# Masked attention with a rational feed-forward: scores as four 64-row products, the exponentials' sums in PSUM, fewer transfers, an order of its own

## The chip, the cores and the metric

The kernel runs on one core of a Trainium2 chip. The metric is device time in microseconds (us). The kernel before was timed three times: 1306.28 us in the median, 1305.25 to 1308.36. Engines are named as in the profile: PE is TensorE, DVE is VectorE, ACT is ScalarE, POOL is GpSimd, SP is SyncE, whose queue issues DMAs.

## The reference

Inputs are q, k and v of shape (8, 8, 576, 64): batch, heads, sequence, head size. All is float32.

```python
scores = scale * np.matmul(q, k.transpose(0, 1, 3, 2))
thresh = np.max(scores, axis=-1, keepdims=True) - tau
scores = np.where(scores >= thresh, scores, -1000000000.0)
scores = scores - np.max(scores, axis=-1, keepdims=True)
attn = np.exp(scores)
attn = attn / (np.sum(attn, axis=-1, keepdims=True) + 1e-09)
attn_out = np.matmul(attn, v)
...
x = np.ascontiguousarray(attn_out.transpose(0, 2, 1, 3)).reshape(B * S, H * D)
h = x @ w_in
P = a[0] + a[1] * h + a[2] * h * h + a[3] * h * h * h
Q = 1.0 + np.abs(b[0]) * np.abs(h) + np.abs(b[1]) * h * h
out = (P / (Q + 1e-06)) @ w_out
```

w_in is (512, 2048), w_out (2048, 512), and x has 4608 rows of 512. Only scores within tau of their row's maximum pass.

## The kernel before

**Units.** Two heads make a pair; there are 4 pairs in a batch and 32 in all. The 576 queries of a pair fall into four full tiles of 128 rows (t = 0 to 3) and a remainder of 64 (t = 4). A full unit is 128 queries of both heads against 576 keys; a remainder unit holds the 64 queries of both heads, one head in each half of the 128 rows. That makes 128 full units and 32 remainder units. A visit is a run of units of one pair: first tiles 0 and 1 of each pair of a batch, then tiles 2, 3 and the remainder on the way back. For each visit the transposed q and k of the pair are loaded into QQ and KK, two buffers of each (`load_ops`).

**A full unit's scores** (`f_qk`, L786 to L809). The first head's 64 channels lie on rows 0 to 63 of QQ and KK, the second head's on rows 64 to 127. Each head takes one product of 64 rows by 512 keys (L805). The last 64 keys of both heads are done in one product over all 128 rows (L809): KK holds two blocks of zeros, so that each head's queries meet only their own keys. The scores fill parts of three PSUM banks: bank 0 and the first 64 columns of bank 1 for the first head, the last 64 columns of bank 1 and bank 2 for the second. A PSUM bank has 512 float32 columns. In the trace a float32 product is two matmuls.

**Behind the scores.** DVE takes the two row maxima (L815). L822 or L824 makes the threshold. ACT reads the scores out of PSUM, head by head, with a function that throws the scores below the threshold far down (L830), and then gives the three banks back: the operation is planned at L956 with the hold on the banks to drop. ACT takes the exponential in SBUF, and the sum of each row with it (L834); the profile shows the reading of that sum as an instruction of its own, ACTIVATION_READ_ACCUMULATOR. The sum goes to a small SBUF tile, st. L839 (on ACT) or L841 (on DVE) scales it, and L845 inverts it. Then the weights are split into a high and a low float16 part (L339/L341 and L856), transposed by a DMA of SP's queue (L866) and multiplied by v (L925). In the first batch the transposes run on TensorE instead (L879, L884, L909).

**Banks.** The first 21 units choose between two sets of banks, (0, 1, 2) and (3, 4, 5); from the 22nd on all have the one set (0, 1, 2). Banks 3 to 5 are then the accumulators and work banks of the feed-forward, 5 to 7 its other work banks.

**Feed-forward.** Steps of 256 rows of x by 512 of the 2048 middle columns (`moe_ops`): L1042 multiplies by w_in, L1051 takes the result out of PSUM, the rational function runs on DVE (L1062 to L1084) and ACT (L1056, L1069, L1072), and L1101 multiplies by w_out. They run beside the score units of later batches, and the last ones by themselves.

**The order** is written out by the program. Each operation is given to a planner (`Plan`) with an engine, or two to choose from, a duration, a key, what it comes after, and what buffers or banks it takes and drops. The planner goes through a model of time, at each step starts the operation that can start soonest, and among those that are level, the one with the smallest key. The keys come from the unit's position, and from two lists of numbers, TURN (one per unit or step) and KIND (one per sort of operation). PRICE and EARLY weigh ACT against DVE where both could do the work. Every engine then does its instructions in the order in which the plan has put them; semaphore waits between engines follow from the tiles that instructions share.

**Loads.** The q and k of the first two batches are issued from SP's queue (k of the first two pairs from ACT's), those from the third batch on from POOL's queue. A q load is three transfers (L650 to L652), a k load is three (L657 to L659), and two more in a visit with a remainder (L662).

Of the kernel before, what the change touches and what calls it, by code (L numbers as in the profile page):

```python
# [16 lines left out]
AX = mybir.AxisListType  # L17

# [27 lines left out]
NQ = 2  # L46
# [4 lines left out]

FROM_ACT = 2
# [25 lines left out]
EARLY = {"ACT": 1.2900, "DVE": 3.3863}  # L78
EARLY_END = 714.5248
PRICE = {"ACT": 1.0645, "DVE": 2.1978}  # L80

TURN = [
# [21 lines left out]
KIND = [  # L104
# [8 lines left out]
LOADS_END = 120.0  # L113
# [22 lines left out]
class Plan:  # L136
# [20 lines left out]
    def op(self, eng, dur, key, fn, after=(), take=(), drop=()):  # L157
        engs = {eng: dur} if isinstance(eng, str) else eng
        o = Op(engs, key, fn, [x for x in after if x is not None], list(take), list(drop))
        o.turn, o.kind = self.turn, self.kinds.setdefault(fn.__code__, len(self.kinds))  # L160
# [26 lines left out]
    def order(self):  # L187
# [19 lines left out]
        left = len(self.ops)  # L207
        while left:
# [38 lines left out]
            if e == "DMA" and o.drop and t < LOADS_END:  # L247

                o.dur = 2.0 * o.dur + 1.0
            free[e] = end = t + o.dur  # L250
            busy[e] += o.dur
            seen = end + self.LAT[e]
            for h in o.take:
# [18 lines left out]
            for d in o.then:  # L272
                d.wait -= 1
                for x in d.engs:
                    d.ready[x] = max(d.ready[x], end + (self.OWN[e] if x == e else self.TO.get((e, x), self.LAT[e])))
                    if not d.wait:
                        can[x].append(d)
# [12 lines left out]
def masked_attention_rational_ffn(  # L290
# [86 lines left out]
    QW = S + REM  # L377
    QQs = [const.tile([P, QW], F32, name=f"QQ{i}") for i in range(NQ)]
    KKs = [const.tile([P, QW + REM], F32, name=f"KK{i}") for i in range(NQ)]
    for t in QQs:  # L380
        nc.gpsimd.memset(t[:, NT * P:], 0.0)
    for t in KKs:
        nc.gpsimd.memset(t[0:D, S:QW], 0.0)
        nc.gpsimd.memset(t[D:P, 0:REM], 0.0)
# [96 lines left out]
    def decode_ops(i, key, load, hold, dst=None):  # L481
# [6 lines left out]
        def ld():  # L488
            if not loaded:

                for x in KKs[0][:, REM:REM + 1], QQs[0][:, 0:1]:
                    nc.gpsimd.tensor_scalar(cf[:, 15:16], x, 1.0, 1.0, ALU.mult, ALU.mult)
# [32 lines left out]
        l = op("GD", 2.5, key - 2.0, ld, (), [hold])  # L525
# [112 lines left out]
    def load_ops(bp, ts):  # L638
# [7 lines left out]
        queue, eng = (nc.sync, "DMA") if bp < EARLY_BP else (nc.gpsimd, "GD")  # L646

        def ldq():
# [3 lines left out]
            queue.dma_start(QQ[D:P, S:], qT[bb, pr, :, S:S + REM])  # L652

        def ldk():
            KK = KKs[kh.slot]
            kq_ = nc.scalar if bp < FROM_ACT else queue
            kq_.dma_start(KK[0:D, REM:S], kT[bb, pr, :, 0:NT * P])  # L657
            kq_.dma_start(KK[D:P, REM:QW], kT[bb, pr, :, S + REM:])
            kq_.dma_start(KK[0:D, 0:REM], kT[bb, pr, :, NT * P:S])  # L659
            if NT in ts:  # L660
                for i in range(2):
                    kq_.dma_start(KK[i * D:(i + 1) * D, QW:], kT[bb, pr, :, NT * P + i * REM:S + i * REM])  # L662

        q_done[bp] = [op(eng, 4.3 if first else 1.6, p0, ldq, (), [qh])]
        k_done[bp] = [op(eng, 0.1 if bp < FROM_ACT else 1.6, p0 + 0.1, ldk, (), [kh])]

# [13 lines left out]
    def load_v_ops(bp):  # L680
# [25 lines left out]
        l = v_loaded[bp] = op(eng, 1.6, max(q, V0 + V1 * pr), ld, (), [vhold])  # L706
# [56 lines left out]
    def unit_ops(bp, t):  # L763
# [3 lines left out]
        single = units.index((bp, t)) < SINGLE  # L767
# [18 lines left out]
        def f_qk():  # L786
# [5 lines left out]
            if not full:  # L792

                s = box["s"][0] = s[:, 0:S]
                for k0, c0, n in (REM, 0, NT * P), (QW, NT * P, REM):
                    nc.tensor.matmul(s[:, c0:c0 + n], QQ[:, NT * P:QW], KK[:, k0:k0 + n], **one)
# [4 lines left out]
            for hh in range(2):  # L801

                r = slice(hh * D, (hh + 1) * D)
# [480 lines left out]
```

## Time and profile before

| | |
|---|---|
| median of three runs | 1306.28 us |
| the profiled execution | 1312.41 us |
| its span, first to last instruction | 1310.6 us |
| mean granted TensorE clock | 0.986 |
| PE busy | 1253.8 us (96%) |
| DVE busy | 1217.9 us (93%) |
| ACT busy | 1114.4 us (85%) |
| POOL busy | 243.4 us (19%) |
| full units' 512-wide products, L805 | 154.0 us, 512 matmuls |
| full units' shared product, L809 | 63.3 us, 256 matmuls |
| exponentials, L834 | 222.1 us, 288; reading their sums 58.1 us, 288 |

Busy time is the union of an engine's instructions. Those of TensorE overlap, and their ends are modelled, so starts tell more than lengths there. In a row of the timeline stand the start, the length, the engine, the line, the operation, what it writes and reads, the shape and the count; in a row of groups the count is followed by busy time, mean ns of one, and the idle time of the engine ahead of them with what ended it.

### The profile page before, as it was taken

To read this page: it belongs to the slowest core of one execution; us is meant where nothing else is said; L and a number is where in the kernel's file an instruction comes from. 1 tells how busy PE (TensorE), PEld (TensorE's weight loads), DVE (VectorE), ACT (ScalarE), POOL (GpSimd) and SP (SyncE) were. 2 spreads that over 40 slices of the span, in tenths; PEclk is the share of its full clock that TensorE was granted. 3 is DMA by queue.
4 is the path that set the end of the run, shared out by engine and by line. 5 is a ranking of instruction groups with operands and counts; after the bars stand their busy time and mean duration, and the time that the engine had idled before them with its cause. 6 is when DMAs were issued, how large, how long until landed. Compare 5 with 4: busy or idle time off the path is not lost. (4 is left out here: it accounts for less than half of the span.)

```text
span 1310.6 us, 25351 instructions
## 1 busy us (share of the span) xinstructions
PE 1253.8 (96%) x9430; PEld 931.8 (71%) x9430; DVE 1217.9 (93%) x1913; ACT 1114.4 (85%) x2182; POOL 243.4 (19%) x462
## 2 busy tenths in 40 slices
PE   8898989999999999998999979999999999999998
PEld 6576677777677777776777657766677777778886
DVE  5899999999999999988999979999999999999777
ACT  5898998999999999997999878978998798885564
POOL 1101100023213220323112231223213221110000
PEclk8998999999999999999999989999999999999999
DMA  7433454476656565677554875676756654563000
GB/s 206 132 116 125 142 128 87 105 160 119 124 116 134 124 131 107 117 143 129 95 103 96 115 132 100 122 126 119 137 106 115 132 131 75 109 111 55 17 17 17
DMA packets 340587, 146.66 MB, mean 112 GB/s; under 512 B 316208, under 2 KB 323184, under 8 KB 340464
## 3 DMA queue, kind: packets, MB, share of 16 engines
q1 hardware_dynamic: 316400, 86.49, 37.4%
q0 software_dynamic: 22784, 57.31, 16.4%
q8 instruction: 74, 1.21, 0.4%
q10 hardware_dynamic: 1280, 1.25, 0.4%
q14 instruction: 49, 0.40, 0.1%
HBM read 60.30 MB, written 9.44 MB: 53 GB/s over the span
## 5 line engine op out<-in xcount | busy, mean ns | idle before, releaser
L1101 PE MATMUL banks<-wp,g 128*128 128x512 f32 x1728 | 442.1, 404 | 1.6 <-DVE g L1092 1.2
L1042 PEld LDWEIGHTS <-wi 128*128 128x128 f16 x3456 | 333.6, 98 | 67.1 <-issue 29.0
L1042 PE MATMUL banks<-x,wi 128*128 128x256 f16 x3072 | 360.8, 274 | 10.0 <-ACT t L1051 9.3
L1101 PEld LDWEIGHTS banks<-wp,g 128*128 128x128 f32 x1728 | 315.9, 189 | 75.3 <-DVE g L1092 4.0
L834 ACT ACTIVATE e<-e,cf 128x576 f32<-128x576 f32 x288 | 222.1, 778 | 0.2
L856 DVE SCALAR_TENSOR_TENSOR e<-e,st,hi 128x576 f16<-128x576 f32 x252 | 204.6, 812 | 7.5 <-ACT hi L339 6.4
L339 ACT ACTIVATE hi<-e,st 128x576 f16<-128x576 f32 x223 | 169.6, 769 | 46.8 <-DVE st L845 30.8
L830 ACT ACTIVATE e<-banks,st 128x576 f32<-128x576 f32 x288 | 206.3, 737 | 3.0 <-DMA pT<-e 0.8
L815 DVE TENSOR_REDUCE st<-banks 128x2 f32<-128x1152 f32 x128 | 172.4, 1347 | 16.2 <-PE banks L809 15.8
L805 PE MATMUL banks<-KK,QQ 64*128 64x512 f32 x512 | 154.0, 650 | 7.2 <-DVE t L346 3.9
L925 PE MATMUL banks<-pT,V 128*64 128x256 f16 (+1 forms) x2520 | 122.8, 250 | 12.8 <-DMA pT<-e 10.2
L1051 ACT ACTIVATE t<-banks,hsc 128x512 f32<-128x512 f32 (+1 forms) x192 | 106.1, 574 | 30.3 <-PE banks L1042 24.5
L925 PEld LDWEIGHTS <-V 128*64 128x64 f16 x2520 | 105.0, 111 | 34.0 <-issue 22.7
L809 PEld LDWEIGHTS banks<-KK,QQ 128*128 128x128 f32 x256 | 38.6, 190 | 99.1 <-issue 94.6
L1078 DVE SCALAR_TENSOR_TENSOR t<-t,co,t 128x1024 f32<-128x1024 f32 (+1 forms) x73 | 92.3, 1265 | 17.4 <-ACT t L1072 17.1
L1069 ACT ACTIVATE t<-t,co 128x1024 f32<-128x1024 f32 (+1 forms) x73 | 82.8, 1134 | 29.6 <-DVE t L1065 24.1
L1092 DVE TENSOR_TENSOR g<-t,g 128x512 fp32r<-128x512 f32 x144 | 95.0, 684 | 3.1 <-ACT g L331 2.9
L650 POOL DMA_DIRECT2D QQ<-in_qT_dram x42 | 22.2, 529 | 381.0 <-PE banks L809 194.8
L1084 DVE SCALAR_TENSOR_TENSOR t<-t,co,t 128x1024 f32<-128x1024 f32 (+1 forms) x73 | 92.3, 1265 | 0.6
L1075 DVE SCALAR_TENSOR_TENSOR t<-t,co,t 128x1024 f32<-128x1024 f32 (+1 forms) x73 | 92.2, 1264 | 0.1
L1065 DVE SCALAR_TENSOR_TENSOR t<-t,co 128x1024 f32<-128x1024 f32 (+1 forms) x73 | 92.3, 1264 | 0.0
L1062 DVE SCALAR_TENSOR_TENSOR t<-t,co 128x1024 f32<-128x1024 f32 (+1 forms) x73 | 92.2, 1263 | 0.0
(128 smaller groups left out, 1545.3 us busy)
## 6 DMA issues: line engine op xcount, KB each, us to landing
t<-in_w_in_dram POOLq DMA_DIRECT2D x16, 512.0 KB, 5.3
t<-in_w_out_dram POOLq DMA_DIRECT2D x16, 512.0 KB, 4.1
out_dram<-u POOLq DMA_DIRECT2D x26, 256.0 KB, 2.9
V<-in_v_dram POOLq DMA_DIRECT2D x24, 256.0 KB, 4.5
QQ<-in_qT_dram POOLq DMA_DIRECT2D x42, 144.0 KB, 2.8
KK<-in_kT_dram POOLq DMA_DIRECT2D x42, 144.0 KB, 3.2
QQ<-in_qT_dram POOLq DMA_DIRECT2D x42, 128.0 KB, 2.9
KK<-in_kT_dram POOLq DMA_DIRECT2D x42, 128.0 KB, 2.8
```

Source lines behind the costliest of these rows:

```text
L339: nc.scalar.activation(dst, src, AF.Identity, scale=factor)
L805: nc.tensor.matmul(d, QQ[r, t * P:(t + 1) * P], KK[r, REM:S], **one)
L815: nc.vector.tensor_reduce(box["st"][:, 0:2], box["both"], AX.X, ALU.max, negate=True)
L830: nc.scalar.activation(ev(hh), box["s"][hh], AF.Prelu, scale=SCALE, bias=box["st"][:, 2 + hh:3 + hh], alpha=STEEP)
L834: nc.scalar.activation(e, e, AF.Exp, scale=passes, accum_out=box["st"][:, 4 + hh:5 + hh])
L856: nc.vector.scalar_tensor_tensor(box["lo"][:, c], ev(hh), box["st"][:, 6 + hh:7 + hh], box["hi"][:, c], ALU.mult, ALU.subtract)
L925: nc.tensor.matmul(dst, V[:, c * P + hh * D:c * P + (hh + 1) * D], rhs, start=c == 0 and n == 0, stop=c == NT and n == 2)
L1042: nc.tensor.matmul(d, wi_tile(c, f0 + j, hl), x[:, c, :], start=c == 0 and n == 0, stop=c == NC - 1 and n == 2)
L1051: nc.scalar.activation(box["h3"][:, 2 * k:2 * k + 2, sl], psv[:, :, sl], AF.Identity, scale=hsc[:, b2, g:g + 1])
L1065: nc.vector.scalar_tensor_tensor(box["q"], box["q"], bc, box["q"], ALU.add, ALU.mult)
L1092: nc.vector.tensor_tensor(fr(g[:, 1]), box["r"][:, k * GW:(k + 1) * GW], g[:, 0], ALU.subtract)
L1101: nc.tensor.matmul(acc[tt], fr(g[:, x]), fr(wo[f][y]), start=begins and j == n == 0, stop=ends and j == nb - 1 and n == 2)
```

## The change

A full unit's scores are made by four products of 64 rows: the first head's last 64 keys (bank 1), the second head's first 512 (bank 2), the first head's first 512 (bank 0), the second head's last 64 (bank 1). Ahead of the last stands an empty instruction on TensorE that waits for the first. KK no longer has blocks of zeros, and its four memsets go. The remainder unit keeps its two products over all rows.

From the 22nd unit on the sum of the exponentials goes to bank 1, in columns 64 to 79, two for each of eight units in turn, and L839/L841 read it from there.

K is loaded by two transfers, one for each head, whole. Q is loaded by two, and a third in visits with a remainder. ACT's queue issues only the first visit's k of the first two pairs. The queues of q and k are as before otherwise: SP for the first two batches, POOL from the third on.

TURN, KIND, EARLY and PRICE have other values. The planner counts a transfer's landing in another way (`wire`), and two durations are other numbers: a full unit's products 1.36 for 1.47, an exponential 0.735 for 0.76.

```diff
-EARLY = {"ACT": 1.2900, "DVE": 3.3863}
+EARLY = {"ACT": 1.2754, "DVE": 3.5364}
-PRICE = {"ACT": 1.0645, "DVE": 2.1978}
+PRICE = {"ACT": 1.0661, "DVE": 2.2744}
...
-    QW = S + REM
-    KKs = [const.tile([P, QW + REM], F32, name=f"KK{i}") for i in range(NQ)]
-    for t in KKs:
-        nc.gpsimd.memset(t[0:D, S:QW], 0.0)
-        nc.gpsimd.memset(t[D:P, 0:REM], 0.0)
+    KKs = [const.tile([P, S], F32, name=f"KK{i}") for i in range(NQ)]
...
+        act = bp < FROM_ACT and ts[0] == 0
-            queue.dma_start(QQ[D:P, S:], qT[bb, pr, :, S:S + REM])
+            if NT in ts:
+                queue.dma_start(QQ[D:P, S:], qT[bb, pr, :, S:S + REM])
...
-            kq_ = nc.scalar if bp < FROM_ACT else queue
-            kq_.dma_start(KK[0:D, REM:S], kT[bb, pr, :, 0:NT * P])
-            kq_.dma_start(KK[D:P, REM:QW], kT[bb, pr, :, S + REM:])
-            kq_.dma_start(KK[0:D, 0:REM], kT[bb, pr, :, NT * P:S])
-            if NT in ts:
-                for i in range(2):
-                    kq_.dma_start(KK[i * D:(i + 1) * D, QW:], kT[bb, pr, :, NT * P + i * REM:S + i * REM])
+            kq_ = nc.scalar if act else queue
+            for hh, c in (0, 0), (1, S + REM):
+                kq_.dma_start(KKs[kh.slot][hh * D:(hh + 1) * D, :], kT[bb, pr, :, c:c + S])
...
-            for hh in range(2):
+            for hh, k0, n, d0 in (0, NT * P, REM, NT * P), (1, 0, NT * P, w - NT * P), (0, 0, NT * P, 0), (1, NT * P, REM, w - S):
                 r = slice(hh * D, (hh + 1) * D)
-                d = s[:, 0:NT * P] if hh == 0 else s[:, w - NT * P:]
-                nc.tensor.matmul(d, QQ[r, t * P:(t + 1) * P], KK[r, REM:S], **one)
-
-            dst, src = (bass.AP(x.tensor, x.offset, [list(x.ap[0]), [n, 2], [1, REM]])
-                        for x, n in ((s[:, NT * P:S], w - 2 * NT * P - REM), (KK[:, 0:REM], S)))
-            nc.tensor.matmul(dst, QQ[:, t * P:(t + 1) * P], src, **one)
+                if d0 == w - S:
+                    tc.add_manual_dep(nc.tensor.nop().ins, shared.ins.name, ORDERED, reason="one bank")
+                mm = nc.tensor.matmul(s[:, d0:d0 + n], QQ[r, t * P:(t + 1) * P], KK[r, k0:k0 + n], **one)
+                if d0 == NT * P:
+                    shared = mm
...
+        def total(h0, h1):
+            if single:
+                return box["st"][:, 4 + h0:4 + h1]
+            o = S - 512 + 2 * (place_of[bp, t] % 8)
+            return ps[:, 1, o + h0:o + h1]
...
-            nc.scalar.activation(e, e, AF.Exp, scale=passes, accum_out=box["st"][:, 4 + hh:5 + hh])
+            nc.scalar.activation(e, e, AF.Exp, scale=passes, accum_out=total(hh, hh + 1))
...
-                nc.scalar.activation(r, box["st"][:, 4:4 + nh], AF.Copy, scale=UP, bias=1e-9 * UP)
+                nc.scalar.activation(r, total(0, nh), AF.Copy, scale=UP, bias=1e-9 * UP)
-                nc.vector.tensor_scalar(r, box["st"][:, 4:4 + nh], 1e-9, UP, ALU.add, ALU.mult)
+                nc.vector.tensor_scalar(r, total(0, nh), 1e-9, UP, ALU.add, ALU.mult)
...
-        qk = op("PE", 1.47 if full else 1.12, p, f_qk, need, [sh[0]], [kh, qh] * nh)
+        qk = op("PE", 1.36 if full else 1.12, p, f_qk, need, [sh[0]], [kh, qh] * nh)
...
-            mk[hh] = op("ACT", 0.76, p + 0.3 + 0.02 * hh, lambda hh=hh: f_sum(hh), [ex[hh]])
+            mk[hh] = op("ACT", 0.735, p + 0.3 + 0.02 * hh, lambda hh=hh: f_sum(hh), [ex[hh]])
```

More of the change, by code (lines that the diff above doesn't have):

```diff
@@ L50 @@
 EARLY_BP = 8
+EARLY_QK = 8
 FROM_ACT = 2
@@ L206, in order @@
         done, busy = [], dict.fromkeys(engines, 0.0)
-        left = len(self.ops)
+        left, wire = len(self.ops), 0.0
         while left:
@@ L252, in order @@
             seen = end + self.LAT[e]
+            if o.wire is not None:
+                wire = max(wire, t + BEGIN) + o.wire[0]
+                seen = max(wire, end + 1.0) + o.wire[1]
             for h in o.take:
@@ L274, in order @@
                 for x in d.engs:
-                    d.ready[x] = max(d.ready[x], end + (self.OWN[e] if x == e else self.TO.get((e, x), self.LAT[e])))
+                    d.ready[x] = max(d.ready[x], seen if o.wire is not None else
+                                     end + (self.OWN[e] if x == e else self.TO.get((e, x), self.LAT[e])))
                     if not d.wait:
@@ L374, in masked_attention_rational_ffn @@
     ones = bass.AP(one.tensor, one.offset, [list(one.ap[0]), [0, P]])
-    QW = S + REM
-    QQs = [const.tile([P, QW], F32, name=f"QQ{i}") for i in range(NQ)]
-    KKs = [const.tile([P, QW + REM], F32, name=f"KK{i}") for i in range(NQ)]
+    QQs = [const.tile([P, S + REM], F32, name=f"QQ{i}") for i in range(NQ)]
     for t in QQs:
         nc.gpsimd.memset(t[:, NT * P:], 0.0)
-    for t in KKs:
-        nc.gpsimd.memset(t[0:D, S:QW], 0.0)
-        nc.gpsimd.memset(t[D:P, 0:REM], 0.0)
+    KKs = [const.tile([P, S], F32, name=f"KK{i}") for i in range(NQ)]
     nc.vector.tensor_scalar(passes, cf[:, 6:7], 0.0, None, ALU.is_ge)
@@ L489, in ld @@
             if not loaded:
-                for x in KKs[0][:, REM:REM + 1], QQs[0][:, 0:1]:
+                for x in KKs[0][:, 0:1], QQs[0][:, 0:1]:
                     nc.gpsimd.tensor_scalar(cf[:, 15:16], x, 1.0, 1.0, ALU.mult, ALU.mult)
@@ L523, in f6 @@
                 tensor_tensor(dst.bitcast(I32), t, box["rw"][:, :, 0], ALU.add)
-        l = op("GD", 2.5, key - 2.0, ld, (), [hold])
+        l = op("GD", 2.5, key - 2.0, ld, (), [hold], wire=(1.75, 2.0))
         if i < NC:
@@ L645, in load_ops @@
         p0 = p - (4.6 if first else 4.0)
-        queue, eng = (nc.sync, "DMA") if bp < EARLY_BP else (nc.gpsimd, "GD")
+        act = bp < FROM_ACT and ts[0] == 0
+        queue, eng = (nc.sync, "DMA") if bp < EARLY_QK else (nc.gpsimd, "GD")
         def ldq():
@@ L651, in ldq @@
             queue.dma_start(QQ[D:P, 0:NT * P], qT[bb, pr, :, S + REM:])
-            queue.dma_start(QQ[D:P, S:], qT[bb, pr, :, S:S + REM])
+            if NT in ts:
+                queue.dma_start(QQ[D:P, S:], qT[bb, pr, :, S:S + REM])
         def ldk():
-            KK = KKs[kh.slot]
-            kq_ = nc.scalar if bp < FROM_ACT else queue
-            kq_.dma_start(KK[0:D, REM:S], kT[bb, pr, :, 0:NT * P])
-            kq_.dma_start(KK[D:P, REM:QW], kT[bb, pr, :, S + REM:])
-            kq_.dma_start(KK[0:D, 0:REM], kT[bb, pr, :, NT * P:S])
-            if NT in ts:
-                for i in range(2):
-                    kq_.dma_start(KK[i * D:(i + 1) * D, QW:], kT[bb, pr, :, NT * P + i * REM:S + i * REM])
-        q_done[bp] = [op(eng, 4.3 if first else 1.6, p0, ldq, (), [qh])]
-        k_done[bp] = [op(eng, 0.1 if bp < FROM_ACT else 1.6, p0 + 0.1, ldk, (), [kh])]
+            kq_ = nc.scalar if act else queue
+            for hh, c in (0, 0), (1, S + REM):
+                kq_.dma_start(KKs[kh.slot][hh * D:(hh + 1) * D, :], kT[bb, pr, :, c:c + S])
+        issue = {"DMA": 1.25, "GD": 1.1}[eng]
+        q_done[bp] = [op(eng, 3.1 if first else issue + (0.6 if NT in ts else 0.0), p0, ldq, (), [qh], wire=(0.75, 1.0))]
+        k_done[bp] = [op(eng, 0.1 if act else issue, p0 + 0.1, ldk, (), [kh], wire=(0.75, 1.0))]
+    place_of = {u: i for i, u in enumerate(units)}
     def is_plain(bp, t):
@@ L705, in load_v_ops @@
         q = bp * (NT + 0.5) - 17.0
-        l = v_loaded[bp] = op(eng, 1.6, max(q, V0 + V1 * pr), ld, (), [vhold])
+        l = v_loaded[bp] = op(eng, 1.7, max(q, V0 + V1 * pr), ld, (), [vhold], wire=(0.95, 1.5 if eng == "DMA" else 2.5))
         hv = [Hold("u", 1)]
@@ L766, in unit_ops @@
         full = t < NT
-        single = units.index((bp, t)) < SINGLE
+        single = place_of[bp, t] < SINGLE
         heads = (0, 1) if full else (0,)
@@ L794, in f_qk @@
                 s = box["s"][0] = s[:, 0:S]
-                for k0, c0, n in (REM, 0, NT * P), (QW, NT * P, REM):
-                    nc.tensor.matmul(s[:, c0:c0 + n], QQ[:, NT * P:QW], KK[:, k0:k0 + n], **one)
+                for c0, n in (0, NT * P), (NT * P, REM):
+                    nc.tensor.matmul(s[:, c0:c0 + n], QQ[:, NT * P:], KK[:, c0:c0 + n], **one)
                 return
@@ L982, in unit_ops @@
             tp = op("DMA", TPD if full else 0.6 * TPD, p + 0.6, lambda: f_tp("hi"), his + two["tp"], [two["pT"]] if t % 2 == 0 else (),
-                    [hi_hold])
-            tp = op("DMA", TPD if full else 0.6 * TPD, p + 0.65, lambda: f_tp("lo"), los + [tp], (), [e_hold])
+                    [hi_hold], wire=(1.2 if full else 0.65, 0.8))
+            tp = op("DMA", TPD if full else 0.6 * TPD, p + 0.65, lambda: f_tp("lo"), los + [tp], (), [e_hold], wire=(1.2 if full else 0.65, 0.8))
             two["tp"].append(tp)
```

10 lines of the change are left out of this document (5 added, 5 removed), and 50 rows, old and new, of tables (KIND, TURN).

## The prediction

> **What bounds the kernel now.** First the page, for the balance of the engines:
>
> ```profile
> span 1310.6 us, 25351 instructions
> ...
> PE 1253.8 (96%) x9430; PEld 931.8 (71%) x9430; DVE 1217.9 (93%) x1913; ACT 1114.4 (85%) x2182; POOL 243.4 (19%) x462
> ...
> DVE 19%; ACT 4%; issue 4%; PE 2%; DMA 1%; ACTq 0%; DVEq 0%
> ```
>
> The chain of waits reaches back only over 30% of the span, and VectorE holds 19 of those 30 parts; but TensorE is as full. So I cut the span into start, middle and tail with the view of busy time by stretch (columns: PE, its weight loads, DVE, ACT, POOL):
>
> ```profile
> 0.00:200.00 200.00, 177.57 (x1232) 130.31 (x1233) 174.38 (x391) 172.37 (x374) 22.52 (x58) 0.96 0.49 139
> 200.00:1200.00 1000.00, 970.75 (x7542) 715.27 (x7542) 959.26 (x1438) 881.63 (x1712) 220.90 (x404) 0.99 0.61 117
> 1200.00:1311.00 111.00, 105.49 (x659) 86.23 (x657) 84.25 (x86) 60.44 (x97) 0.00 (x0) 1.00 0.05 15
> ```
>
> In the 1000 us in which score units and feed-forward steps run side by side, TensorE is idle for 29 us, VectorE for 41, ScalarE for 118. Two engines have next to no slack, all work in the order that the program wrote, and a new wait of a microsecond per unit finds no room. What one unit does there, by the timeline of each engine (start, length):
>
> ```profile
> 600.34 0.30 ACT L822 ACTIVATE st<-st,cf 128x2 f32<-128x2 f32 x1
> 600.67 1.37 ACT L830 ACTIVATE e<-banks,st 128x576 f32<-128x576 f32 x2
> 601.93 0.77 ACT L834 ACTIVATE e<-e,cf 128x576 f32<-128x576 f32 x1
> 602.60 0.20 ACT L834 ACTIVATION_READ_ACCUMULATOR e<-e,cf 128x1 f32 x1
> 602.69 0.77 ACT L834 ACTIVATE e<-e,cf 128x576 f32<-128x576 f32 x1
> 603.36 0.19 ACT L834 ACTIVATION_READ_ACCUMULATOR e<-e,cf 128x1 f32 x1
> 603.45 1.14 ACT L1069 ACTIVATE t<-t,co 128x1024 f32<-128x1024 f32 x1
> ```
>
> ```profile
> 602.84 1.13 PE L805 MATMUL banks<-KK,QQ 64*128 64x512 f32 x4
> 603.90 0.49 PE L809 MATMUL banks<-KK,QQ 128*128 128x128 f32 x2
> 604.14 2.34 PE L1101 MATMUL banks<-wp,g 128*128 128x512 f32 x9
> ```
>
> ```profile
> 604.49 0.16 DVE L841 TENSOR_SCALAR st<-st 128x2 f32<-128x2 f32 x1
> 604.69 0.17 DVE L845 RECIPROCAL st<-st 128x2 f32<-128x2 f32 x1
> 604.77 1.34 DVE L815 TENSOR_REDUCE st<-banks 128x2 f32<-128x1152 f32 x1
> ```
>
> From the 22nd unit on there is one set of score banks (0, 1, 2). ScalarE empties it with L830 (ends 602.04); the next unit's products enter it at 602.84, while the exponentials of the unit before still run (the second ends at 603.55) and before its sums are read (L841, 604.49). Today that is free, since the sums lie in an SBUF tile.
>
> **The change, part by part.**
>
> *Sums in bank 1.* The exponential of unit n (L834) now writes its sum into bank 1, into which unit n+1's two 64-wide products write and from which its maximum reads; L839/L841 read the sum from there. The diff itself makes one of the 64-wide products wait for the other, with the reason "one bank"; I take it that sums and products, which share that bank on two engines, are kept in program order as well. Then a product that stands behind the sums in the program waits for them, and a sum that stands behind the product waits for the product. How often would they meet? Over 138 successions of units on the single set, I compared the start of a unit's first product with the end of the sums before it: in 121 the product is the earlier, by 0.83 us in the median and 127 us in all. The first and the last:
>
> ```profile
> 171.34 1.35 PE L805 MATMUL banks<-KK,QQ 64*128 64x512 f32 x4
> ```
>
> ```profile
> 174.40 0.83 ACT L834 ACTIVATE e<-e,cf 128x576 f32<-128x576 f32 x1
> 175.06 0.25 ACT L834 ACTIVATION_READ_ACCUMULATOR e<-e,cf 128x1 f32 x1
> ```
>
> ```profile
> 1179.35 1.19 PE L796 MATMUL banks<-KK,QQ 128*128 128x512 f32 x4
> ```
>
> ```profile
> 1179.37 0.76 ACT L834 ACTIVATE e<-e,cf 128x576 f32<-128x576 f32 x1
> 1180.04 0.19 ACT L834 ACTIVATION_READ_ACCUMULATOR e<-e,cf 128x1 f32 x1
> ```
>
> Bounds of the wait on TensorE: none, where the new order keeps them apart; 127 us, where every product stands behind both sums. In between: if a product that now starts before the second sum stands ahead of that sum in the program, it waits for the first alone. By the same comparison that makes 75 us on TensorE, and 64 us on ScalarE for the second sums that then wait for the product. I take 75, because the planner's list knows nothing of this wait: the score banks are still given back by L830 (the hold that L956 drops), and the exponential takes no hold on them. Queued behind the waiting product on TensorE are the feed-forward matmuls (L1101 from 604.14 above), and VectorE's L1062 to L1092 wait for those. TensorE's own 29 us of idle time take some of it; ScalarE's 64 us fit into its 118. On the path: 75 - 29 = +46 us (bounds 0 and 127).
> The Trainium skill, page "PSUM — Partial Sum Buffer", section "PSUM bank collisions raise a hardware error", says that accesses by two engines have to be guarded by bank and quarter of the partitions, and not by address, reads included. By that rule the different columns of the sums are no protection, and the wait is certain; by addresses alone it would be nothing. No row here shows two engines on different columns of one bank.
>
> *Four products.* Today a full unit takes TensorE from 602.84 to 604.14, 1.30 us; before a feed-forward step of the other layer it is 1.39:
>
> ```profile
> 194.33 1.13 PE L805 MATMUL banks<-KK,QQ 64*128 64x512 f32 x4
> 195.39 0.49 PE L809 MATMUL banks<-KK,QQ 128*128 128x128 f32 x2
> 195.72 0.38 PE L1042 MATMUL banks<-x,wi 128*128 128x256 f16 x2
> ```
>
> A float32 product is two passes; the 64-row pairs run side by side, four records in 1.06 us, 0.53 a pass. The new unit has on each half of the rows two 512-wide passes and two 64-wide ones. No row shows a 64-row, 64-wide pass. The nearest is the remainder unit on all rows:
>
> ```profile
> 244.40 0.65 PE L796 MATMUL banks<-KK,QQ 128*128 128x512 f32 x2
> ```
>
> ```profile
> 243.97 1.19 PE L796 MATMUL banks<-KK,QQ 128*128 128x512 f32 x4
> 245.00 0.38 PE L1042 MATMUL banks<-x,wi 128*128 128x256 f16 x2
> ```
>
> There a 512-wide pass takes 0.43, and the two 64-wide ones what is left of 1.03: 0.17, or 0.085 each. If the 64-row form adds the 0.10 that it adds to a 512-wide pass, 0.185. So the new unit takes 1.06 + 0.17 to 1.06 + 0.37, 1.23 to 1.43, against 1.30 to 1.39: from -0.11 to +0.08 a unit, times 128 units -14 to +10 us. I take the middle, -2. The wait for the first 64-wide product is over long before the other half has done its 1.06 us.
> The Trainium skill, page "TensorE: Matmul & The Clock Gate", part "Packing small matmuls — row/col tiling", says that a weight load overlaps running matmuls only on other rows. The 0.53 against 0.43 agrees, and by that rule the part would gain nothing.
>
> *The sum's own price.* A pass with a sum takes 0.76 (601.93 to 602.69), one without 0.69 (half of 1.37): at most 0.07 times 288 = 20 us of ScalarE's time, at least nothing. I take 8, and on the path -1, since ScalarE has 118 us to spare. The 45 sums read on VectorE may cost as much more as the nearest small bank read does:
>
> ```profile
> 608.80 0.23 DVE L941 SCALAR_TENSOR_TENSOR xr<-banks,xr 128x64 f16<-128x64 f32 x1
> ```
>
> 0.23 against 0.16, 45 times: +3 us of VectorE, +1 on the path.
>
> *Fewer transfers.* K goes from three or five issues a visit to two, Q from three to two, three in a visit with a remainder; on GpSimd:
>
> ```profile
> L662 POOL DMA_DIRECT2D KK<-in_kT_dram x48 | 26.0, 552 | 0.2 <-issue 0.2
> L652 POOL DMA_DIRECT2D QQ<-in_qT_dram x42 | 22.7, 540 | 0.0
> L659 POOL DMA_DIRECT2D KK<-in_kT_dram x42 | 22.5, 535 | 1.8 <-DMA V<-in_v_dram 1.7
> ...
> L650 POOL DMA_DIRECT2D QQ<-in_qT_dram x42 | 22.2, 529 | 381.0 <-PE banks L809 194.8 <-PE banks L796 181.8 <-PE banks L1101 4.4
> ```
>
> Of these the 48, the 42 of L659 and 18 of L652 go, some 58 us of issuing, but the queue stood idle for 381 us ahead of L650 until TensorE gave a buffer back: hidden by the visit in work, two buffers deep. Without that cover it would be about two issues, 1.1 us, for each of 42 visits. In the first batch the second visits of two head pairs move from ScalarE's queue to SP's, and on GpSimd four memsets of K go:
>
> ```profile
> 1.34 0.61 ACTq L658 DMA_DIRECT2D KK<-in_kT_dram  x1
> 1.48 0.59 SPq L650 DMA_DIRECT2D QQ<-in_qT_dram  x1
> 1.54 0.14 POOL L383 MEMSET KK<- 64x64 f32 x1
> ...
> 8.41 1.13 PE L805 MATMUL banks<-KK,QQ 64*128 64x512 f32 x4
> ```
>
> Ten issues of 0.61 leave ScalarE in the first 200 us (28 us idle there), four of 0.59 join SP, where transposes queue behind them; the memsets lie seven microseconds ahead of the first product. All of it together I count as -1 us (bounds -6, all ten issues on the path, and +2, the four on SP's).
>
> *Own order.* Bounds from the idle time: it can win back at most TensorE's 29 us and lose any amount; I take -2.
>
> **Sum.** 46 - 2 - 1 + 1 - 1 - 2 = +41 on the span of 1310.6, 1351.6. The profiled execution took 1312.4, 1.8 more than its span, and the median of the runs is 1306.3, 0.5% below it: (1351.6 + 1.8) x 0.9953 = 1347; I say 1345.
>
> **The rivals.**
> *Kept apart (faster).* Place: the bank between L830 and the next product. The new order puts other matmuls ahead of each product and the sums straight behind L830, so no wait is seen, and the products and the sums' price give what they can: -14 and half of the 8, 1288; two thirds of it, 1294. For it: in 17 of 138 successions the sums are over in time already. Against: the list does not know that they must be. It decides once the waits for sums stay under the 29 us that TensorE has to spare.
> *Full chain (far slower).* Every product stands behind both sums, and bank 1 goes from product to maximum to L830 to sums and back, one owner at a time: 127 - 29 - 5 = +93, 1399. For it: L834 starts straight behind L830 in the rows above, and so stands early in the program. It decides where the product is planned later than the second sum in most units; today that is 74 of 138.
> *Products in file.* If the passes start only in program order, the second head's last wide pass starts at 0.53, the first head's two wide passes behind it at 0.53 and 1.06, and the unit ends near 1.6 instead of 1.30 to 1.39: +0.21 to 0.3, times 128 at least +27 us: 1333, with no wait for sums. The four records in 1.06 speak against it, since two pairs ran side by side, with the first head's second pass behind the second head's first. The Trainium skill's page on TensorE, in the part named above, says that matmuls start and end in program order, which would be this case if it held for each pass.
> *Nothing.* The change is off the path at both ends: 1306.
>
> **How the numbers follow.** Forecast (waits for the sums, 1310 to 1375 by itself) 0.38; full chain 0.11; in file 0.06: slower 0.55. Kept apart 0.38: faster. Nothing 0.07: same. A change under 0.2% can't be told from none. The range 1291 to 1390 leaves out the best of "kept apart" and the worst of "full chain".
>
> **What would show it.** Right: L805's first product preceded by idle time on TensorE that ends with ScalarE's L834, some 0.5 us each, tens of us in all; or L834 preceded by idle time that ends with TensorE's products. Wrong: neither row, with L830 still followed by L834 within 0.1 us and TensorE's idle time between 200 and 1200 us still near 29. The four products: 1.23 to 1.43 us to the next matmul, 1.6 if in file. A sum's pass below 0.76 shows its price. POOL's idle time ahead of its Q transfers stays in the hundreds.

## The result, and the profile after

The changed kernel takes 1432.32 us (median of four runs, 1428.70 to 1436.69) beside 1305.76 for the kernel before: a ratio of 1.0967 with a 95% interval of 1.0932 to 1.1002, or 127 us more. The forecast was 1345, with a range that ended at 1390. It had the sign, and the size was missed threefold. The changed file has other line numbers: the four products are L807, the remainder's L797, the exponential L840, the sums' scaling L845 (ACT) and L847 (DVE), the reciprocal L851, the feed-forward's products L1048 and L1107.

The page of the changed kernel first, its span, engines and chain of waits:

```profile
span 1430.2 us, 25976 instructions
...
PE 1266.7 (89%) x9716; PEld 977.4 (68%) x9716; DVE 1223.8 (86%) x1918; ACT 1129.6 (79%) x2178; POOL 185.6 (13%) x349
...
PE 14%; ACT 9%; DVE 6%; issue 4%; DMA 1%; POOL 1%; ACTq 0%; DVEq 0%; POOLq 0%
```

The work hardly grew: TensorE 13 us more than before, VectorE 6, ScalarE 15. The span grew by 120. So it is idle time, and the view of busy time by stretch (columns as in the prediction) shows that all engines have it:

```profile
200.00:1200.00 1000.00, 878.41 (x6845) 667.85 (x6843) 857.95 (x1283) 803.87 (x1536) 155.42 (x282) 0.97 0.54 105
```

In the same 1000 us, into which less of the work now fits, TensorE idles for 122 us (29 before), VectorE for 142 (41), ScalarE for 196 (118). Each idles for another 80 to 100 us, and so does ScalarE, which had four times TensorE's idle time to begin with.

The view of waits names who stood for whom (total us, times, longest):

```profile
ACT e L840 <- PE banks L807: 88.6, 63, 2.7
PE banks L807 <- ACT e L840: 82.2, 72, 4.2
DVE st L851 <- ACT st L845: 44.3, 51, 2.2
ACT st L845 <- PE banks L807: 35.9, 29, 2.4
DVE st L847 <- ACT e L840: 34.8, 22, 3.7
```

Both of the prediction's signs are there, and at once: products wait for exponentials (82 us), exponentials wait for products (89 us). ScalarE's and VectorE's reading of the sum, and the reciprocal, wait behind them. In the groups (busy us, mean ns, then idle time ahead with what ended it) the exponential's row was, before the change:

```profile
L834 ACT ACTIVATE e<-e,cf 128x576 f32<-128x576 f32 x288 | 222.1, 778 | 0.2
```

Its row now, and that of the four products:

```profile
L840 ACT ACTIVATE e<-e,cf 128x576 f32<-128x576 f32 x288 | 224.3, 780 | 105.6 <-PE banks L807 88.6 <-PE banks L797 12.0
L807 PE MATMUL banks<-KK,QQ 64*128 64x512 f32 (+1 forms) x1024 | 180.5, 464 | 104.3 <-ACT e L840 82.2 <-ACT e L830 18.8 <-DVE st L847 1.7
```

One succession in the timeline, ScalarE, TensorE and VectorE picked out of one window (start, length, idle time ahead and what ended it):

```profile
1014.84 0.78 ACT L840 ACTIVATE e<-e,cf 128x576 f32<-128x576 f32 x1
1015.52 0.15 ACT L840 ACTIVATION_READ_ACCUMULATOR e<-e,cf 128x1 f32 x1
...
1015.72 1.52 PE L807 MATMUL banks<-KK,QQ 64*128 64x64 f32 x8 [2.29 <-ACT e L840]
...
1017.34 0.78 ACT L840 ACTIVATE e<-e,cf 128x576 f32<-128x576 f32 x1 [1.67 <-PE banks L807]
...
1018.20 0.17 ACT L845 ACTIVATE st<-banks 128x2 f32<-128x2 f32 x1
1018.27 1.26 ACT L1057 ACTIVATE t<-banks,hsc 128x512 f32<-128x512 f32 x2
1018.40 0.17 DVE L851 RECIPROCAL st<-st 128x2 f32<-128x2 f32 x1 [1.03 <-ACT st L845]
...
1019.00 1.23 PE L1048 MATMUL banks<-x,wi 128*128 128x256 f16 x5 [1.76 <-ACT t L1057]
```

The next unit's products stand in the program behind the first head's sum and ahead of the second's. So TensorE is idle for 2.29 us until the first sum is written (1015.67), works through all four products, and only then may ScalarE start the second exponential, after 1.67 us of idling. Behind that on ScalarE stands L1057, which empties a feed-forward bank; TensorE, finished at 1017.24, waits for it until 1019.00. One unit stops TensorE twice. In 40 full units the trace has both waits: the products held by one sum, and the next exponential held by those products.

### The profile page after: what moved, and what is told of

It reads as the page before. It is cut to its first block, busy times and chain, and to the rows that moved or that the text cites. A ratio compares the mean times of both kernels' runs of the same rounds, so it can differ in the third digit from the quotient of the medians.

```text
span 1430.2 us, 25976 instructions
## 1 busy us (share of the span) xinstructions
PE 1266.7 (89%) x9716; PEld 977.4 (68%) x9716; DVE 1223.8 (86%) x1918; ACT 1129.6 (79%) x2178; POOL 185.6 (13%) x349
## 5 line engine op out<-in xcount | busy, mean ns | idle before, releaser
L1107 PE MATMUL banks<-wp,g 128*128 128x512 f32 x1728 | 454.8, 409 | 14.2 <-DVE g L1098 7.7
L1048 PEld LDWEIGHTS <-wi 128*128 128x128 f16 x3456 | 333.0, 99 | 80.7 <-issue 36.1
L1107 PEld LDWEIGHTS banks<-wp,g 128*128 128x128 f32 x1728 | 316.8, 191 | 97.3 <-DVE g L1098 15.4
L1048 PE MATMUL banks<-x,wi 128*128 128x256 f16 x3072 | 367.4, 276 | 13.3 <-ACT t L1057 12.0
L840 ACT ACTIVATE e<-e,cf 128x576 f32<-128x576 f32 x288 | 224.3, 780 | 105.6 <-PE banks L807 88.6
L807 PE MATMUL banks<-KK,QQ 64*128 64x512 f32 (+1 forms) x1024 | 180.5, 464 | 104.3 <-ACT e L840 82.2
L807 PEld LDWEIGHTS banks<-KK,QQ 64*128 64x128 f32 x1024 | 117.9, 191 | 183.1 <-ACT e L840 109.8
L1057 ACT ACTIVATE t<-banks,hsc 128x512 f32<-128x512 f32 (+1 forms) x192 | 106.0, 577 | 21.5 <-PE banks L1048 19.3
L660 POOL DMA_DIRECT2D KK<-in_kT_dram x84 | 43.9, 526 | 519.2 <-PE banks L807 265.4
```

Source lines behind the costliest of these rows:

```text
L807: mm = nc.tensor.matmul(s[:, d0:d0 + n], QQ[r, t * P:(t + 1) * P], KK[r, k0:k0 + n], **one)
L840: nc.scalar.activation(e, e, AF.Exp, scale=passes, accum_out=total(hh, hh + 1))
L1048: nc.tensor.matmul(d, wi_tile(c, f0 + j, hl), x[:, c, :], start=c == 0 and n == 0, stop=c == NC - 1 and n == 2)
L1057: nc.scalar.activation(box["h3"][:, 2 * k:2 * k + 2, sl], psv[:, :, sl], AF.Identity, scale=hsc[:, b2, g:g + 1])
L1107: nc.tensor.matmul(acc[tt], fr(g[:, x]), fr(wo[f][y]), start=begins and j == n == 0, stop=ends and j == nb - 1 and n == 2)
```

## The experiments

**Only the sums moved back.** The changed kernel with its own order, products and transfers, the sums in st for all units.

```diff
-            if single:
+            if True:
```

> The changed kernel with the exponentials' sums back in the SBUF tile for all units; four products, transfers and order as changed. Theory 'shared bank' (the time went into waits between a unit's sums and the next unit's products): all 126 us come back, 1290 to 1310, and no idle time of ScalarE ahead of the exponentials that ends with a product. Rival 'order' (the new order, made with other durations, costs the time): stays above 1400. Rival 'products' (four products or the wait between them cost it): stays above 1400 as well, with more than 1.4 us from a unit's first product to the next matmul.

1304.85 us; 0.9992 (0.9968 to 1.0017) of the kernel before. All 127 us go with this one edit. The groups and the stretch of this kernel:

```profile
L840 ACT ACTIVATE e<-e,cf 128x576 f32<-128x576 f32 x288 | 221.5, 776 | 0.2
L807 PE MATMUL banks<-KK,QQ 64*128 64x512 f32 (+1 forms) x1024 | 177.4, 458 | 33.6 <-ACT e L830 33.1 <-DMA QQ<-in_qT_dram 0.3
```

```profile
200.00:1200.00 1000.00, 962.85 (x7779) 749.75 (x7778) 957.67 (x1441) 890.45 (x1709) 163.12 (x296) 0.99 0.60 116
```

No exponential waits any more, and the idle times are back at 37, 42 and 110 us. Everything else in the change together is worth nothing that can be measured.

**Only the sums moved away.** The kernel before, with `total()` of the change (the sums in bank 1) and nothing else.

> The kernel before with one thing changed: from the 22nd unit on the sums go to bank 1. Order, products and transfers are those of before. 'Shared bank': 1400 to 1450, with ScalarE waiting for products and products waiting for exponentials, some 100 us each. 'Order' and 'products': within 10 us of before.

1358.24 us; 1.0393 (1.0362 to 1.0423), where 1400 or more was expected. So the sums cost 52 us here and 127 in the changed kernel. The groups of this one (L805 the 512-wide products, L809 the shared one behind them):

```profile
L840 ACT ACTIVATE e<-e,cf 128x576 f32<-128x576 f32 x288 | 224.2, 779 | 72.4 <-PE banks L809 58.6 <-PE banks L796 7.7 <-DVE st L815 1.1
L805 PE MATMUL banks<-KK,QQ 64*128 64x512 f32 x512 | 163.7, 647 | 8.7 <-DMA QQ<-in_qT_dram 5.1 <-ACT e L830 3.1
L809 PE MATMUL banks<-KK,QQ 128*128 128x128 f32 x256 | 62.8, 327 | 5.3 <-ACT e L840 5.1
```

And from the view of waits the weight loads of the shared product:

```profile
PEld banks L809 <- ACT e L840: 61.0, 72, 1.4
```

The shared product waits for a sum in 72 units, but the 512-wide ones run meanwhile, so that TensorE's idle time ahead of it is 5 us. What sticks out lengthens a unit, from its first product to the next other matmul, from 1.41 us to 1.57. These are means of the 102 to 104 units that lie behind 200 us, that the timeline shows whole, and whose next matmul doesn't wait. In the 111 full units from the 22nd on that makes some 18 us, the 5 among them; the remainder units' products (L796) wait another 7 us for sums. So TensorE loses some 25 us directly. ScalarE waits 66 us for products, and the other 27 of the 52 are put down to those waits by subtraction. A part of them is seen: the feed-forward's first products wait longer for ScalarE's emptying of their bank (L1051 before, L1057 in this kernel). Before the change, and with the sums alone:

```profile
L1042 PE MATMUL banks<-x,wi 128*128 128x256 f16 x3072 | 360.8, 274 | 10.0 <-ACT t L1051 9.3 <-DVE x L941 0.4
```

```profile
L1048 PE MATMUL banks<-x,wi 128*128 128x256 f16 x3072 | 363.9, 275 | 20.3 <-ACT t L1057 18.7 <-DVE x L947 0.9 <-ACT st L845 0.4
```

**Only the four products, and with the fewer transfers.** The kernel before with the change's product loop over KK as it was laid out before (first edit below), and then with the change's KK, QQ and their loads as well, in the order of before.

```diff
-            for hh in range(2):
+            for hh, k0, n, d0 in (0, 0, REM, NT * P), (1, REM, NT * P, w - NT * P), (0, REM, NT * P, 0), (1, S, REM, w - S):
```

> The kernel before with the four products alone (K's layout, transfers, order and sums as before). By the trace of the changed kernel a unit's products take 1.28 us to the next matmul in place of 1.30 to 1.39, so up to 128 times 0.1 = 13 us of TensorE: 1293 to 1306. 'Products' as the cause: 1330 or more.

> The kernel before with the four products and the fewer transfers; sums and order as before. If the transfers are hidden, equal to the kernel with the four products alone within 3 us. Against the changed kernel with its sums put back it differs by the order alone: 'order' as a cause says this one is more than 20 us faster than that one; 'shared bank' says within 10 us.

1302.37 us, 0.9967 (0.9946 to 0.9988), and 1301.70 us, 0.9968 (0.9949 to 0.9987). The products gain 4 us; the transfers add nothing to it. The second is faster than both kernels: the change without its sums and its order.

**The sums of every second unit.** The changed kernel, with bank 1 for every other unit.

```diff
-            if single:
+            if single or place_of[bp, t] % 2:
```

> The changed kernel with the sums of every second unit back in the SBUF tile, the rest in bank 1. A price for each unit, paid alone: half of the 127 us that the sums cost in that order, 1360 to 1375. If late units push the next ones into waiting (the price grows with how many there are): under 1355.

1367.22 us, 1.0484 (1.0439 to 1.0529): 62 of the 127 us for half of the units. The price is paid unit by unit: it isn't one price for using the bank at all, and slack doesn't swallow the first half of it.

**A bank of their own.** The changed kernel with the sums in bank 7, which is taken from the feed-forward's work banks (first), and the same with that bank taken and the sums in st (second).

```diff
-[(7,), (6,), (5,)]
+[(6,), (5,)]
...
-            return ps[:, 1, o + h0:o + h1]
+            return ps[:, 7, o + h0:o + h1]
```

> The changed kernel with the sums in bank 7, which is taken from the feed-forward's and the transposes' work banks (they keep banks 5 and 6), so that no product writes the sums' bank. 'Shared bank': the waits between sums and products go; 1300 to 1330, the upper part for the missing work bank. If the sums' being in PSUM as such is what costs (a slower write or read there): above 1380.

> The control of the run with the sums in bank 7: bank 7 is taken from the work banks in the same way, but the sums go to the SBUF tile. If the missing work bank alone made that run slow, and sums in a bank that nobody else writes cost nothing: within 10 us of 1409. If sums in PSUM cost something by themselves: 1300 to 1380.

1409.04 us, 1.0799 (1.0743 to 1.0855), and 1411.91 us, 1.0809 (1.0750 to 1.0867). Against its control the sums in PSUM cost nothing: the intervals cover each other. The missing work bank costs about 105 us, which is why the first alone would mislead. The exponentials of the first, and its reading of the sums, then the reading of the second:

```profile
L840 ACT ACTIVATE e<-e,cf 128x576 f32<-128x576 f32 x288 | 223.6, 777 | 3.7
...
L840 ACT ACTIVATION_READ_ACCUMULATOR e<-e,cf 128x1 f32 x288 | 48.2, 167 | 0.0
```

```profile
L840 ACT ACTIVATION_READ_ACCUMULATOR e<-e,cf 128x1 f32 x288 | 57.1, 198 | 0.0
```

Same exponential, same PSUM, another bank: the waits fall from 105.6 to 3.7 us. It is the sharing of bank 1.

**A planner that knows.** The changed kernel, with the single set of banks given back only when the sums have been read.

```diff
-        sh = dict.fromkeys(heads, Hold("s", nh, B2 if single else B3))
+        sh = dict.fromkeys(heads, Hold("s", nh + (not single), B2 if single else B3))
...
-        rec = op(FLEX["rec"], 0, p + 0.4, f_rec, list(mk.values()))
+        rec = op(FLEX["rec"], 0, p + 0.4, f_rec, list(mk.values()), (), () if single else [sh[0]])
```

> The changed kernel with the planner told that the score banks come back only when the sums have been read (the hold is dropped by that operation, not by L830 alone); lists, products and transfers as changed, so the order comes out another. If what costs is that the order was made without knowing of the wait: well under 1432, 1310 to 1370, with no waits between sums and products. If one set of banks held that long is itself the limit: 1390 or more, with TensorE waiting elsewhere.

1445.78 us, 1.1078 (1.1042 to 1.1113): slower still. The exponentials' waits are gone, and the wait for the next unit's maximum takes their place:

```profile
ACT st L822 <- DVE st L815: 68.6, 47, 8.1
```

```profile
L840 ACT ACTIVATE e<-e,cf 128x576 f32<-128x576 f32 x288 | 224.0, 779 | 7.5
```

That wait was 23 us before the change and 20 in the changed kernel. So this plan around the same sharing is no cure: the one set of banks is now held longer for each unit, and the time goes there. TURN and KIND are those of the change; lists made for this plan were not run.

**Which of the other edits turns 52 into 127.** The sums and the four products, on the order and transfers of before; then with the transfers too.

> The kernel before with the four products and the sums in bank 1; transfers and order as before. If the transfers take no part: 1395 to 1410, as with them. If the transfers are what turns 1358 into 1402: 1350 to 1370.

> The kernel before with all three changes (four products, transfers, sums in bank 1) but in its own old order, with its old durations and lists. 'Place of bank 1's products': near the changed kernel, 1410 to 1450. 'Order': near the kernel with the sums alone, 1345 to 1370.

1407.91 us, 1.0786 (1.0749 to 1.0824), and 1402.48 us, 1.0757 (1.0716 to 1.0798). The transfers have no part in it. With the four products the sums cost 1402.48 - 1301.70 = 101 us, with the old ones 52: the products double it. The groups of the second (L832 the exponential, L799 the products) show both directions of the wait in the old order too:

```profile
L832 ACT ACTIVATE e<-e,cf 128x576 f32<-128x576 f32 x288 | 224.0, 779 | 98.4 <-PE banks L799 84.9 <-PE banks L790 7.5 <-DVE st L807 1.1
L799 PE MATMUL banks<-KK,QQ 64*128 64x512 f32 (+1 forms) x1024 | 176.1, 455 | 78.2 <-ACT e L832 70.5 <-DMA QQ<-in_qT_dram 3.2 <-ACT e L822 2.0
```

The own order adds the last 30 us (1432 against 1402), though without the sums it is level with the old one (1304.85 against 1301.70).

**Why the products double it: place, or both ends?** Before, bank 1 is written only by the last product of a unit. The four products write it with the first and with the last. Three kernels move the products of bank 1 to one place. In the first, the two that write bank 1 are both last, in the changed kernel; in the second, both first, in the kernel with products, transfers and sums on the old order:

```diff
+            for hh, k0, n, d0 in (1, 0, NT * P, w - NT * P), (0, 0, NT * P, 0), (0, NT * P, REM, NT * P), (1, NT * P, REM, w - S):
```

> The changed kernel with the four products in another order: the two 512-wide ones first (banks 2 and 0), the two 64-wide ones of bank 1 last; all else as changed, sums in bank 1. With the sums alone in the kernel before, the wait fell on the shared product, which is the last of its unit, so its first microsecond ran under the wait; in the changed kernel the first product is one of bank 1. Theory 'place of bank 1's products': 1350 to 1390, though the last product then waits for the one just ahead of it (some 0.2 us a unit, up to 28 us). Rival 'order' (the new order meets the sums more often): 1430 as before, give or take 15.

```diff
+            for hh, k0, n, d0 in (0, NT * P, REM, NT * P), (1, NT * P, REM, w - S), (0, 0, NT * P, 0), (1, 0, NT * P, w - NT * P):
```

> The kernel before with all three changes in its old order (1402 with the 64-wide products at the two ends of a unit), and now with both 64-wide products first, then the two 512-wide. Theory 'both ends': with one product of bank 1 at the unit's start and one at its end, the unit waits for the sums at its start and the second sum waits for its end, so both waits are paid; in one place only one is: 1355 to 1385, near the 1358 of the kernel with one shared product, plus up to 0.2 us a unit for the wait between the two. Rival 'tighter all round' (TensorE's shorter units only leave less idle time to hide the waits in, or the transfers take part): 1395 or more.

1423.29 us, 1.0917 (1.0877 to 1.0957), and 1401.10 us, 1.0730 (1.0686 to 1.0773): no gain to speak of, where less than 1390 was expected of both; the second meets what its rival had named, 1395 or more. But a unit itself grew. The second's, from the timeline:

```profile
1071.68 1.83 PE L799 MATMUL banks<-KK,QQ 64*128 64x64 f32 x8
1073.45 0.72 PE L1040 MATMUL banks<-x,wi 128*128 128x256 f16 x5
```

From its first product to the next matmul there are 1.77 us, the median of all units too, against 1.28 in the kernel with the products alone: 0.49 more in each of 128 units, 63 us of TensorE's time, which is more than the 44 us between 1402 and the 1358 with one place. In the first it is 1.72. The sums are not what lengthens it: in the first 160 us, where they still go to st, the medians are the same (1.78 in the second, 1.72 in the first). The two neighbouring 64-wide products, of which one waits for the other, no longer have a 512-wide one beside them. The waits for sums did fall. These are TensorE's weight loads for the products, in the view of waits, first in the changed kernel and in the first of the two:

```profile
PEld banks L807 <- ACT e L840: 109.8, 81, 4.5
PEld banks L807 <- ACT e L840: 47.6, 80, 1.4
```

Then on the old order, with the products at both ends and in the second of the two:

```profile
PEld banks L799 <- ACT e L832: 98.0, 85, 2.6
PEld banks L799 <- ACT e L832: 65.0, 81, 2.3
```

With both products in one place the loads wait about as long as with the one shared product (61 us above). ScalarE's waits for products fell less, from 89 to 85 us and from 85 to 62. And these two kernels have no control with the sums in st, so their times can't tell what the sums cost in them. The third leaves the old shared product as it is and issues it first (the kernel before with the sums, and the product of L809 moved ahead of those of L805):

> The kernel before with the sums in bank 1 and its shared product (bank 1) issued ahead of the two 512-wide ones; nothing else. 'Place of bank 1's products': 1400 to 1450, against 1358 with the shared product last. 'Order': within 15 us of 1358.

1359.25 us, 1.0424 (1.0385 to 1.0463): the same as with it last, where 1400 or more was expected. Its groups:

```profile
L840 ACT ACTIVATE e<-e,cf 128x576 f32<-128x576 f32 x288 | 224.4, 780 | 49.1 <-PE banks L803 29.4 <-PE banks L796 13.5 <-DVE st L815 1.1
L803 PE MATMUL banks<-KK,QQ 128*128 128x128 f32 x256 | 60.6, 319 | 51.3 <-ACT e L840 40.4 <-ACT t L507 5.6 <-ACT e L830 1.7
```

With the shared product first, TensorE waits more (40 us for sums, where it was 5) and ScalarE less (43 us for products, where it was 66): the wait changes sides and the price stays. So one place costs 52 to 55 us, whichever it is.

Then both ends, without the four products: the old shared product cut into two full-row products of 64 columns, one ahead of the 512-wide ones and one behind, no wait between them; with the sums in bank 1, and as its control with the sums in st.

```diff
+            nc.tensor.matmul(s[:, NT * P:S], q, KK[:, 0:REM], **one)
...
-            nc.tensor.matmul(dst, QQ[:, t * P:(t + 1) * P], src, **one)
+            nc.tensor.matmul(s[:, w - S:w - NT * P], q, KK[:, S:QW], **one)
```

> The kernel before with the sums in bank 1 and its shared product cut in two over all rows, the first head's last 64 keys ahead of the two 512-wide products, the second head's behind them. Bank 1 is then written at both ends of a unit without four 64-row products and without a wait between products. 'Both ends': the sums cost about 100 us against the control, 1400 or more if the control is near 1306. 'Something else in the four products': about 52 us against the control.

> Control of the run with the shared product cut in two: the same products, sums in SBUF. A unit has two full products of 64 columns in place of one of 128, some 0.1 us more on TensorE: 1306 to 1320.

1462.49 us, 1.1207 (1.1175 to 1.1239), and 1321.65 us, 1.0120 (1.0093 to 1.0146): the sums cost 141 us, where about 100 was expected. The groups of the one with sums (L802 the product ahead, L807 the one behind):

```profile
L838 ACT ACTIVATE e<-e,cf 128x576 f32<-128x576 f32 x288 | 224.0, 778 | 125.2 <-PE banks L807 111.1 <-PE banks L796 8.1 <-DVE st L813 1.1
L802 PE MATMUL banks<-KK,QQ 128*128 128x64 f32 x256 | 53.6, 291 | 85.7 <-ACT e L838 74.1 <-DMA V<-in_v_dram 5.3 <-ACT t L1116 2.1
```

The product ahead waits for the sums before it, and the sum behind waits for the last product: both waits at full size, with no 64-row product in bank 1. So the doubling needs nothing of the four products but that a unit touches bank 1 at both ends. That it is the two ends, and not just a second product in that bank, rests on the weight loads' waits above (110, 98 and, here, 104 us with both ends; 48 to 65 with one place); a run that shows it in the time is missing.

## Why the prediction was right in sign and wrong in size

**The sums in bank 1: right mechanism, wrong price.** The reason was borne out by the sums moved back, moved alone, and put into a bank of their own: sums and products at different columns of bank 1 are kept in program order, both ways. The rule quoted from the Trainium skill, page "PSUM — Partial Sum Buffer", section "PSUM bank collisions raise a hardware error", agrees with that: waits of 82 and 89 us in bank 1, 3.7 us of idle time ahead of the exponentials in a bank of their own. What the chip would do without these waits, no run here shows.

**The step that failed** is "75 - 29 = +46", with "ScalarE's 64 us fit into its 118". Three things in it:

- *The waits were counted with the products of before, whose first product doesn't write bank 1.* The comparison of L805's start with the end of the sums asked when a unit's first product begins, but in that kernel only its last product touches the bank. In the changed loop the first does, and the last does again: the diff showed this in the `d0` of its four tuples. So the count fits the changed kernel only, where TensorE's wait of 82 us (87 with the remainder units) is near the 75 forecast. ScalarE's was taken too small: 64 forecast, 101 measured (89 for L807, 12 for L797); the sum behind a product is held until the last of the four ends. By the runs the price is 52 us with one end, 101 with both (products) or 141 (two full-row products). (The 0.83 us given for the 121 earlier products is the median of all 138 successions; that of the 121 is 0.92.)
- *ScalarE's waits were set against ScalarE's idle time.* The kernel with the sums alone refutes that most directly. TensorE lost some 25 us there and not 75, since bank 1 is touched only by the last product, a microsecond into the unit; ScalarE waited 66 us, as forecast, and by the forecast's accounting these were free. The time rose by 52. That +46 is near it is chance: it was made of the wrong wait. A wait on ScalarE holds L1057 behind it, TensorE waits for that, and the idle time that ScalarE has elsewhere can't be moved to where the wait falls. Where both engines wait, the time grew by two thirds to three quarters of the two waits together: 127 of 171 us in the changed kernel, 101 of 155 on the old order, 141 of 185 with the two full-row products.
- *TensorE's own 29 us were subtracted.* In the changed kernel TensorE's idle time in the stretch is 122, its 29 and 93 more, and nothing shows that any of the 29 was taken up. The sums of every second unit speak against it: half of the units cost half of the price, where slack that took up the first 29 us would have left them less.

**The upper bound of 127 us** is the number measured, by coincidence. It stood for every product waiting for both sums; in fact 72 products and 63 sums waited in turn, 171 us on two engines that partly overlap. The rival *full chain* (1399) comes nearest in size, and the planner that knows, which comes nearest to building it, gives 1446: the bank does go round from owner to owner, but in the changed kernel that happens with a product in between the two sums and not behind both.

**Four products: -2 forecast, -4 measured** (1302.37). 1.28 us to the next matmul (in the median, where the units of before have 1.38) lies in the forecast's 1.23 to 1.43, and *products in file* (1.6) is wrong. That is 13 us less of TensorE's time in 128 units, near the best of the forecast's bounds (14); 4 of them show in the time. The timeline of the kernel with the products alone:

```profile
1043.88 1.34 PE L806 MATMUL banks<-KK,QQ 64*128 64x64 f32 x8
1045.15 4.11 PE L1041 MATMUL banks<-x,wi 128*128 128x256 f16 x36
```

The Trainium skill's page "TensorE: Matmul & The Clock Gate", part "Packing small matmuls — row/col tiling", was read as "no gain"; the small gain goes a little past it. Its sentence on program order, taken pass by pass, would have given the rival's 1.6; here the eight passes take 1.27 us.

**The sum's own price** came out near the forecast in size, but in another instruction. The forecast took 8 us off ScalarE's exponentials, because a pass with a sum would get shorter. With 776 to 780 ns the exponential costs what it did; it is the reading of the sum that is shorter into PSUM, 163 ns instead of 202, 11 us of ScalarE's time. The reading by VectorE costs no more than before:

```profile
L840 ACT ACTIVATION_READ_ACCUMULATOR e<-e,cf 128x1 f32 x288 | 47.0, 163 | 0.0
...
L847 DVE TENSOR_SCALAR st<-banks 128x2 f32<-128x2 f32 (+1 forms) x35 | 5.5, 158 | 46.5 <-ACT e L840 34.8 <-PE banks L807 10.7 <-ACT u L344 0.7
```

158 ns, where 161 was measured before and 230 was taken; but its 46.5 us of idle time ahead are VectorE's share of the sharing.

**Fewer transfers** did what was said: GpSimd's busy time fell from 243.4 to 185.6 us, by the forecast's 58, and its queue still stands idle ahead of the K load until TensorE gives a buffer back, so nothing of it is seen in the time. Two counts were off, without effect: ScalarE's queue issued 16 transfers of k before and 4 now, twelve fewer and not ten, and SP's queue, which was to gain four, went from 42 to 24. GpSimd's K load:

```profile
L660 POOL DMA_DIRECT2D KK<-in_kT_dram x84 | 43.9, 526 | 519.2 <-PE banks L807 265.4 <-PE banks L797 236.0 <-issue 17.7
```

**Own order: -2 forecast.** Without the sums it is worth nothing (1304.85 against 1301.70, within the intervals); with them it costs 30 us. Its places for products and exponentials were not chosen with that wait in view, but neither were those of the old order, and which of its moves costs the 30 us stays open.

**The rivals.** *Kept apart* asked that the order alone keep sums and products apart; neither the old order nor the new does. *Nothing* is wrong.

## What to carry to other kernels

When an edit makes two engines share a bank, write down for one unit every instruction that touches it, in program order, and price each change of owner in both directions; the instruction that touches it first and the one that touches it last set how long it is locked. Don't pay such a wait out of an engine's idle time: here, where the engines go in order and wait for one another, a wait on the one with slack was passed on to the one without. And before a result is put down to a new place for data, run the control that changes the room alone: a bank taken away cost 105 us here, nearly as much as the sharing did.

## What was not expected of the hardware

- With two neighbouring products of 64 columns, on different halves of the rows and in one bank, with a wait of one for the other, a unit takes 1.72 or 1.77 us in place of 1.28; with the 512-wide ones between them the same wait costs nothing that is seen. How much of the 0.44 to 0.49 us is the wait itself is not separated.
- A 64-row product of 64 columns is cheap when others run beside it: all eight passes of a unit take 1.27 us where the four 512-wide ones took 1.06 and the shared one the rest of 1.30.
- Writing the exponential's sum to PSUM is faster than to SBUF, 163 against 202 ns.
- TensorE's granted clock was 0.97 in the stretch with the waits and 0.99 without them (the third figure from the end in the rows by stretch). So a slightly lower clock went with the waits; of the 127 us it can be only a small part, as TensorE's busy time grew by 13.
